# Attention blocks of 256 and 320 tokens across chunk borders in a fused attention and feed-forward kernel on one Trainium2 core

## The chip, the cores and the metric

The kernel runs on one core of one Trainium2 chip. The metric is the device time of one launch in microseconds (us); lower is better. Engines are named as the profile names them: PE is the matrix engine (PEld its weight loads), DVE the vector engine, ACT the scalar engine, POOL the GpSimd engine, and SP the queue that starts nearly all DMA transfers.

## The reference: what is computed

Attention over 8 batches, 8 heads, 576 tokens, head size 64, with keys and values first averaged over groups of eight tokens (72 pooled keys per head), and behind it a feed-forward layer over the 4608 tokens:

```python
k_p = k.reshape(B, H, Sp, pool, D).mean(axis=3)      # Sp = 72
v_p = v.reshape(B, H, Sp, pool, D).mean(axis=3)
attn = softmax(scale * q @ k_p^T)                    # 576 x 72 per head
x = (attn @ v_p), heads side by side                 # 4608 x 512
h = x @ w_in                                         # 4608 x 2048
g = h * erf(softplus(h))
out = g @ w_out                                      # 4608 x 512
```

The softmax is written here as one word; the reference has the maximum, the exponential and the sum spelled out. All is float32.

## The kernel before, in words

**Chunks and batches.** The feed-forward layer works on nine chunks of 512 tokens (`TC`), the attention on eight batches of 576. The two do not divide each other, so `blocks()` (L95) cuts the tokens of a batch into attention blocks of at most 256 tokens which end at a batch end and at a chunk end as well. That gives 24 blocks: 12 of 256 tokens, four of 192, four of 128 and four of 64. A block is made of tiles of 128 or 64 tokens.

**Attention.** `job` (L495) emits one block. Once per batch it loads and pools keys and values (L505 to L515). For each tile, `softmax_tile` loads the queries (L563), splits them into a high and a low part (L566, L571), multiplies with the keys on PE (L579, L581 or L603), does the softmax on DVE and ACT (L585 to L651), and turns the weights on PE (L658, L665) into the block's tiles `eth`, `etl` and `etb`. When all tiles of the block are there, four head pairs follow, and for each of them `values` (L690) issues **four matmuls as wide as the block** (L695), each with its own weights. The result is copied by ACT or DVE into the token buffer of the chunk (L701, L703; in chunks 0 and 1 L707, L709).

**Feed-forward.** Chunks 0 and 1 go straight: `gemm1` (L794, 12 matmuls of 512 columns for 128 of the 2048 features). From chunk 2 on (`FROM`) a Strassen scheme takes its place: `factors` (L465) makes seven combinations of the tokens of a chunk (L475, L480), `sums` (L431) makes combinations of the weights once, during chunk 1, and stores them in DRAM, and `products` (L716) reloads them through a ring of pieces of on-chip memory (L724), four pieces to two steps, and multiplies (L740, 42 matmuls of 256 columns for two steps). DVE and ACT add the products up (L758, L761, L770). Then softplus and erf on ACT (L812, L819; each switch of function loads a table), the product (L822), the split into `gh` and `gl` (L824, L829), and `gemm2` (L843, 12 matmuls of 512 columns a step). A chunk has 16 steps; `store` (L853) writes it out.

**Where things lie.** The 16 pieces `wi0` to `wi15` first hold `w_in`. When chunk 1 has used a piece, it is lent out: tokens of a chunk (`XF`), differences (`TD`), the running sum (`UU`), the sums of every other pair (`HS`), output rows (`OUT`), and the rest is the ring. With `after` an operation is held back until the first holder of its piece is done. At the start the weights come as 64-bit floats and are turned into two 32-bit parts each (`load_weights`, L370 to L408), which takes ACT, DVE and POOL; `gh`, `gl`, `hs` and the weight pieces are lent to the first batches meanwhile.

**What sets the order.** Nothing is written in its final order. Each operation has a priority in steps (`prio`) and an estimated cost, and `Program.order` (L189) places them one by one on the engines, the earliest start first with `SLACK` for priority, none more than `WINDOW` steps ahead of what PE has reached, and only if a buffer is free in the model. Some operations may go to one of several engines (`alt`). Every engine then runs its list in order. Where the model sees PE idle at the start, it puts in matmuls whose result nothing uses (L898, the fillers). The constants L39 to L76 are the priorities: of the weights (`W_IN`, `W_OUT`, `LEAD`), of pooled keys and values (`KEYS`, `VALS`), of the tiles of chunk 0 (`T0`, `T0_STEP`), of gemm2 (`G2`), of the ring (`RING_LEAD`), of `sums` (`SUMS`).

Of the kernel before, what the change touches and what calls it, by code (L numbers as in the profile page):

```python
# [37 lines left out]

WINDOW = 8  # L39
SHIFT = 3  # L40
B1 = 2
T0, T0_STEP = -10.5, 0.45
VAL_R = 2.1
KEYS, KEYS_R, KEYS_S = -5.5, 0.4, -0.5
VALS, VALS_R, VALS_S = -1.0, 0.4, -1.1
Q_DUE = 5.2
W_IN, W_OUT = 1.4, 0.1
LEAD = 4.25
G2 = 5.2
ON_DVE = 2  # L50
# [44 lines left out]
def blocks():  # L95


    out, qo = [], 0
    for b in range(B):
        t = 0  # L100
        while t < S:
            ck, off = divmod(b * S + t, TC)
            n, tiles, fresh = min(256, S - t, TC - off), [], t == 0
            for at in range(0, n, P):
                T = min(P, n - at)
                tiles.append((qo, T))
                qo += P * NP * T
            out.append((ck, b, tiles, off, fresh))
            t += n
    return out  # L110


class Buf:
# [25 lines left out]
class Program:  # L139
# [14 lines left out]
    def op(self, eng, cost, prio, fn, reads=(), writes=(), hold=(), alt=None, funcs=None, port=False):  # L154
# [135 lines left out]
def moe_attention(ctx: ExitStack, tc: tile.TileContext, cst, qa, kl, vl, wi, wo, out):  # L290
# [3 lines left out]
    if wide:  # L294
# [63 lines left out]
    def late(tag, shape, dtype=F32):  # L358
        return Buf(weights, [P] + shape, dtype, tag, [tag])
# [135 lines left out]
    def job(ck, b, tiles, off, times, first, fresh):  # L495

        base, due = times[0], times[-1] + VAL_R
        if fresh:
# [33 lines left out]
            for i in range(2):  # L532
# [150 lines left out]

        xk = xkept(ck) if ck >= FROM else xtile(ck)
        xs = slice(off, off + n)
        for p in range(NP):
# [11 lines left out]
            op("PE", 4 * max(n / 2.4 + 13, 112), r, values, [eth, etl, etb, VA, VB], [pv])  # L698
            if ck >= FROM:
                x = xk[p // 2]  # L700
                after(op("ACT", act(n, True), r + 0.4, lambda p=p, pv=pv, x=x: nc.scalar.copy(  # L701
                    x.ap[:, p % 2, xs], pv.ap[:, :n]), [pv], [(x, (p, off))],
                    alt=("DVE", dve(n), lambda p=p, pv=pv, x=x: nc.vector.tensor_copy(  # L703
                        x.ap[:, p % 2, xs], pv.ap[:, :n]))), w_in[p // 2])
                continue
            x = xk[p]
            op("ACT", act(n, True), r + 0.4, lambda x=x, pv=pv: nc.scalar.copy(  # L707
                x.ap[:, 0, xs], pv.ap[:, :n]), [pv], [(x, (0, off))])
            op("DVE", dve(n), r + 0.5, lambda x=x, pv=pv: nc.vector.tensor_sub(  # L709
                x.ap[:, 1, xs], pv.ap[:, :n], f32(x.ap[:, 0, xs])), [pv, (x, (0, off))], [(x, (1, off))])  # L710

    po = {}

    common, outs = late(UU, [4, HALF]), late(OUT, [2, DM])

    def products(n, unit, hs):  # L716
# [43 lines left out]
        multiply(n, b1, (left, "A11", "B11", True), (right, "S2", "T2", False))  # L760
        after(op("ACT", act(HALF, True), n + 0.6, lambda: nc.scalar.copy(u.ap[:, j], b1.ap[:, lo]), [b1], [(u, j)]), w_in[5])  # L761
# [4 lines left out]
        after(add(n + 0.8, c22, u0, b2, hi, [(u, j)], [(hs[1], 1)]), w_in[4])  # L766
        add(n + 0.85, c22, c22, b2, lo, [(hs[1], 1)], [(hs[1], 1)])
# [175 lines left out]
```

## Time and profile before

| | |
|---|---|
| median of 3 runs | 925.52 us (924.41 to 925.95) |
| the profiled execution, its own time | 921.54 us |
| its span, first to last instruction | 919.7 us |
| PE clock granted, mean | 0.998 |
| HBM traffic | 151.06 MB read, 24.12 MB written |

The span leaves out 1.84 us around the profiled execution. That execution was 3.98 us faster than the median of the runs. Busy times of PE are those of pipelined matmuls, so a matmul's duration is longer than its turn on the array; the distance from one start to the next is what counts.

### The profile page before, as it was taken

Reading aid. Unit: us, or ns where it says so; the run is one execution under the profiler, and the core shown is the slowest. Engines: PE = TensorE matmul, PEld = TensorE weight load, DVE = VectorE, ACT = ScalarE, POOL = GpSimd, SP = SyncE. Lnnn points to the kernel's source line nnn. Section 1 sums busy time; section 2 is a strip of 40 time slices with the busy share of each in tenths; the row PEclk is TensorE's granted clock in tenths of the full one; section 3 lists DMA queues with packets and bytes.
Section 4 is the critical chain, followed back from the end, with each engine's and each line's share of the span. In section 5 each row is a group of like instructions: output and inputs, shape, how many; then the busy total and the mean of one; then the engine's idle time right before and its main releaser. Section 6 shows DMA issues by size and latency. Waiting matters only on the chain.

```text
span 919.7 us, 16168 instructions
## 1 busy us (share of the span) xinstructions
PE 905.8 (98%) x5640; PEld 802.5 (87%) x5640; DVE 654.3 (71%) x1350; ACT 677.7 (74%) x1196; POOL 387.7 (42%) x499
## 2 busy tenths in 40 slices
PE   8999999999999999999999999999999999999998
PEld 7878788788889899999999889899998999989996
DVE  7997894889977687758667677767767866664442
ACT  4799995888668678777677777777776776766754
POOL 3679985555453345426540534344442400221000
PEclk9999999999999999999999999999999999999999
DMA  9981235256587656755665466655865365447511
GB/s 327 405 326 37 72 104 172 104 195 211 182 301 238 196 165 231 252 186 186 198 249 184 143 206 222 217 170 178 269 212 177 134 211 172 150 156 243 180 58 47
DMA packets 68257, 176.24 MB, mean 192 GB/s; under 512 B 11216, under 2 KB 13392, under 8 KB 68176
## 3 DMA queue, kind: packets, MB, share of 16 engines
q1 hardware_dynamic: 67888, 174.69, 55.8%
q8 instruction: 45, 0.74, 0.3%
q10 hardware_dynamic: 288, 0.52, 0.2%
q14 instruction: 36, 0.29, 0.1%
HBM read 151.06 MB, written 24.12 MB: 190 GB/s over the span
## 4 chain that ended last, share of the span: by engine, by line
PE 75%; DVE 6%; ACT 3%; POOL 2%; DMA 2%; issue 1%; POOLq 0%; ACTq 0%; DVEq 0%
PE banks L843 36%; PE banks L740 29%; PE banks L695 3%; PE banks L794 3%; PE banks L579 1%; PE banks L658 1%; DVE hs L822 1%; DMA w<-t 1%; PE banks L581 1%; PE banks L603 1%; ACT L812 1%; DMA wi<-w 1%; ACT y L812 1%; POOL gl L829 0%; DMA out<-f 0%
## 5 line engine op out<-in xcount | busy, mean ns | idle before, releaser
L843 PE MATMUL banks<-wo,gh 128*128 128x512 f32 x1152 | 363.8, 397 | 1.7 <-POOL wo L408 1.5
L740 PE MATMUL banks<-t,wi 128*128 128x256 f32 x2352 | 313.5, 285 | 1.9 <-DVE wi L758 1.4
L740 PEld LDWEIGHTS banks<-t,wi 128*128 128x128 f32 x2352 | 301.2, 191 | 13.4 <-DVE wi L758 2.3
L843 PEld LDWEIGHTS banks<-wo,gh 128*128 128x128 f32 x1152 | 203.9, 189 | 36.1 <-POOL wo L408 2.6
L843 PE MATMUL banks<-wo,gl 128*128 128x512 f32 x576 | 224.8, 390 | 0.0
L843 PEld LDWEIGHTS banks<-wo,gl 128*128 128x128 f32 x576 | 108.2, 188 | 23.9
L812 ACT ACT_TABLE_LOAD x72 | 92.4, 1283 | 29.5 <-DVE hs L758 13.2
L758 DVE TENSOR_TENSOR wi<-wi,banks 128x256 f32<-128x256 f32 x168 | 67.3, 413 | 37.6 <-PE banks L740 19.3
L794 PE MATMUL banks<-t,wi 128*128 128x512 f32 x384 | 93.0, 393 | 0.4 <-DVE y L822 0.4
L511 POOL TENSOR_TENSOR raw<-raw 128x256 f32<-128x256 f32 (+1 forms) x60 | 47.9, 800 | 88.5 <-DMA raw<-vl 38.4
L794 PEld LDWEIGHTS banks<-t,wi 128*128 128x128 f32 x384 | 70.9, 188 | 15.5 <-DVE y L822 0.8
L819 ACT ACTIVATE y<-y 128x1024 f32<-128x1024 f32 (+1 forms) x73 | 76.3, 1046 | 0.7
L819 ACT ACT_TABLE_LOAD x59 | 75.7, 1283 | 1.1
L569 POOL TENSOR_TENSOR ql<-raw,qh 128x512 fp32r<-128x512 f32 (+1 forms) x36 | 42.4, 1177 | 65.1 <-PE banks L843 13.2
L824 ACT CAST gh<-hs 128x512 fp32r<-128x512 f32 x72 | 44.3, 616 | 34.3 <-PE banks L843 25.2
L829 POOL TENSOR_TENSOR gl<-hs,gh 128x512 fp32r<-128x512 f32 x26 | 34.7, 1341 | 77.1 <-ACT gh L824 74.9
L822 DVE TENSOR_TENSOR hs<-y,hs 128x512 f32<-128x512 f32 x72 | 51.5, 750 | 10.8 <-ACT y L819 10.7
L829 POOL TENSOR_TENSOR gl<-wi,gh 128x512 fp32r<-128x512 f32 x20 | 25.9, 1295 | 70.7 <-ACT gh L824 51.1
L822 DVE TENSOR_TENSOR wi<-y,wi 128x512 f32<-128x512 f32 x56 | 38.0, 716 | 20.5 <-ACT y L819 20.5
L829 DVE TENSOR_TENSOR gl<-hs,gh 128x512 fp32r<-128x512 f32 x46 | 35.2, 768 | 23.1 <-ACT gh L824 22.9
L824 ACT CAST gh<-wi 128x512 fp32r<-128x512 f32 x56 | 34.3, 616 | 20.5 <-PE banks L843 13.0
L758 DVE TENSOR_TENSOR hs<-wi,banks 128x256 f32<-128x256 f32 x84 | 32.7, 416 | 22.4 <-PE banks L740 21.5
(163 smaller groups left out, 1540.8 us busy)
## 6 DMA issues: line engine op xcount, KB each, us to landing
wi<-w SPq DMA_DIRECT2D x168, 512.0 KB, 4.2
wi<-w SPq DMA_DIRECT2D x56, 256.0 KB, 4.0
raw<-vl SPq DMA_DIRECT2D x36, 256.0 KB, 3.7
wi<-wi SPq DMA_DIRECT2D x16, 512.0 KB, 8.8
wo<-wo SPq DMA_DIRECT2D x16, 512.0 KB, 8.2
w<-t SPq DMA_DIRECT2D x16, 512.0 KB, 3.4
raw<-kl SPq DMA_DIRECT2D x26, 288.0 KB, 3.4
raw<-qa SPq DMA_DIRECT2D x28, 256.0 KB, 3.9
```

The lines of the kernel that those rows point to most:

```text
L511: op("POOL", gps(4 * size), prio, lambda: nc.gpsimd.tensor_add(t.ap[:, 0:4], t.ap[:, 0:4], t.ap[:, 4:8]), [t], [t])
L569: return e.tensor_sub(ql.ap[:, :, :T], raw.ap[:, :, :T], f32(qh.ap[:, :, :T]))
L695: nc.tensor.matmul(d, w, e, start=(i == 0), stop=(i == 3), skip_group_check=True)
L740: nc.tensor.matmul(dst(), weight(name, w, p), x[:, xl, p, :], start=(first and p == 0 and q == 0), stop=(p == 1 and q == 2), skip_group_ch ...
L758: return op("DVE", dve(HALF), prio, lambda: nc.vector.tensor_add(dst(), x(), b.ap[:, side]), reads + [b], writes)
L794: nc.tensor.matmul(ph.ap, w_in[ft].ap[:, w, P * p:P * p + P], xs[p].ap[:, x], start=(p == 0 and q == 0), stop=(p == NP - 1 and q == 2))
L812: nc.scalar.activation(y.ap[:, half(k)], hh[k].ap, AF.Softplus)
L819: op("ACT", act(w), n + 1.9, lambda sl=sl: nc.scalar.activation(y.ap[:, sl], y.ap[:, sl], AF.Erf), own, own, funcs="sigmoid")
L822: op("DVE", dve(TC), n + 1.9, lambda k=k: nc.vector.tensor_mul(g(k), y.ap[:, half(k)], hh[k].ap), [(y, k), hh[k]], [gs[k]], port=kept)
L824: op("ACT", act(TC), n + 2.0, lambda k=k: nc.scalar.copy(gh[k].ap, g(k)), [gs[k]], [gh[k]], port=True, alt=("DVE", 0.52 * TC + 150, lambda ...
L829: return e.tensor_sub(gl[k].ap, g(k), f32(gh[k].ap))
L843: nc.tensor.matmul(o[t].ap, g.ap[:, gs], w_out[ft].ap[:, w], start=(ft == 0 and q == 0), stop=(ft == NJ - 1 and q == 2))
```

## The change

Four things are changed together, and with them the constants that set priorities.

1. **Blocks.** From the third batch on (`WHOLE = 2`) a batch has two blocks, one of 256 tokens and one of 320 (128 + 128 + 64), wherever the chunk borders lie. `eth`, `etl` and `etb` grow to 320 columns (`BLOCK`). A block that lies across a border is copied out of PSUM in two parts, each to the buffer of its own chunk (`parts`). 24 blocks become 18.
2. **Token buffers.** Two pairs instead of one: `wi0`, `wi1` for even chunks and `wi2`, `wi3` for odd ones. `TD` moves to `wi4`, `UU` to `wi13`, `OUT` to `wi15`, and the two `HS` share `wi14` (the class `Part`). The ring has eight pieces, `wi5` to `wi12`, instead of nine.
3. **`gl`** has two buffers instead of three, which pays for the wider tiles.
4. **Times.** A new loop, last batch first, pulls the tiles' priorities earlier, so that the last tile of a block lies `SHIFT + 4` steps ahead of its chunk and tiles lie at least `CLOSE` = 2 steps apart. The window, the priorities of the weights, of pooled keys and values, of the sums and of the ring change.

```diff
-WINDOW = 8
+WINDOW = 16
-T0, T0_STEP = -10.5, 0.45
-VAL_R = 2.1
-KEYS, KEYS_R, KEYS_S = -5.5, 0.4, -0.5
-VALS, VALS_R, VALS_S = -1.0, 0.4, -1.1
+T0, T0_STEP = -10.5, 0.55
+VAL_R = 4.0
+KEYS, KEYS_R, KEYS_S = -6.5, 0.4, -0.7
+VALS, VALS_R, VALS_S = -0.5, 0.4, -0.7
-W_IN, W_OUT = 1.4, 0.1
-LEAD = 4.25
-G2 = 5.2
+W_IN, W_OUT = 0.9, -0.8
+LEAD = 4
+G2 = 5.0
-SLACK, BIAS = 30, 1150
+SLACK, BIAS = 34, 1150
-RING = tuple(f"wi{i}" for i in range(7, NJ))
-XF, TD, UU, HS, OUT = ("wi0", "wi1"), "wi2", "wi5", ("wi3", "wi4"), "wi6"
-SUMS, SUMS_R = 4.3, 0.3
+RING = tuple(f"wi{i}" for i in range(5, 13))
+XF, TD, UU, HS, OUT = ((0, 1), (2, 3)), 4, 13, 14, 15
+WHOLE, CLOSE, BLOCK = 2, 2.0, 320
+SUMS, SUMS_R = 0.5, 2.3
-RING_LEAD = 6.25
+RING_LEAD = 7.25
...
             n, tiles, fresh = min(256, S - t, TC - off), [], t == 0
+            if b >= WHOLE:
+                n = S - t if t else 256
...
-             "s": 2, "m": 2, "z": 2, "bb": 1, "ks": 1, "vs": 1, "hs": 3, "y": 1, "f": 2, "gh": 3, "gl": 3}
+             "s": 2, "m": 2, "z": 2, "bb": 1, "ks": 1, "vs": 1, "hs": 3, "y": 1, "f": 2, "gh": 3, "gl": 2}
...
-            xf[ck] = [late(XF[i], [2, TC]) for i in range(2)]
+            xf[ck] = [late(f"wi{i}", [2, TC]) for i in XF[ck % 2]]
...
-        r = NJ * (FROM - 1) + 2 * i + SUMS
+        r = NJ * (FROM - 1) + SUMS_R * i + SUMS
...
-        xk = xkept(ck) if ck >= FROM else xtile(ck)
-        xs = slice(off, off + n)
+        parts, at = [], 0
+        while at < n:
+            k, o = divmod(TC * ck + off + at, TC)
+            w = min(n - at, TC - o)
+            parts.append((k, slice(o, o + w), slice(at, at + w)))
+            at += w
...
+    soon = None
+    for ck, b, tiles, off, times, _, _ in reversed(jobs):
+        for i in reversed(range(len(tiles))):
+            if b >= WHOLE:
+                times[i] = min(times[i], NJ * ck - 4 - SHIFT - CLOSE * (len(tiles) - 1 - i))
+                if soon is not None:
+                    times[i] = min(times[i], soon - CLOSE)
+                soon = times[i]
```

Since the order is computed, three places of it are shown as it stands before and after.

PE, batch 3, before: the 64 tokens at the end of chunk 3 (`eth`, `etl`, `etb` are turned softmax weights, `vah`, `val`, `vb` pooled values). Two of the four head pairs:

```order
L695 MATMUL banks<-eth,vah 128x64
L695 MATMUL banks<-etl,vah 128x64
L695 MATMUL banks<-eth,val 128x64
L695 MATMUL banks<-etb,vb 64x64
L843 MATMUL banks<-wo_1655,gh 128x512 x2
L843 MATMUL banks<-wo_1655,gl 128x512
L843 MATMUL banks<-wo_1655,gh 128x512 x2
L843 MATMUL banks<-wo_1655,gl 128x512
L695 MATMUL banks<-eth,vah 128x64
L695 MATMUL banks<-etl,vah 128x64
L695 MATMUL banks<-eth,val 128x64
L695 MATMUL banks<-etb,vb 64x64
```

PE, the same place after: the same 64 tokens and the 256 that follow them in chunk 4 (L714 is the former L695, L866 the former L843, L762 the former L740):

```order
L714 MATMUL banks<-eth,vah 128x320
L714 MATMUL banks<-etl,vah 128x320
L714 MATMUL banks<-eth,val 128x320
L714 MATMUL banks<-etb,vb 64x320
L866 MATMUL banks<-wo_1532,gh 128x512 x2
L866 MATMUL banks<-wo_1532,gl 128x512
L866 MATMUL banks<-wo_1532,gh 128x512 x2
L866 MATMUL banks<-wo_1532,gl 128x512
L762 MATMUL banks<-t,wi_3949 128x256 x6
L714 MATMUL banks<-eth,vah 128x320
L714 MATMUL banks<-etl,vah 128x320
L714 MATMUL banks<-eth,val 128x320
```

What were two blocks with 16 matmuls each is one block with 16 wider ones.

POOL at the start, before: from the first pair's `gl` to the low part of the second `w_out` piece, `wo1` (L332 and L408 are conversions, L390 the low bits of a weight):

```order
L829 TENSOR_TENSOR gl_1038<-y_933,gh_1031 128x512
L829 TENSOR_TENSOR gl_1048<-y_933,gh_1042 128x512
L332 TENSOR_SCALAR wo0_1080<-f_1050 128x512
L390 TENSOR_SCALAR hs_1085<-wi5_646 128x512
L408 TENSOR_TENSOR wo0_1080<-f_1050,wo0_1080 128x512
L675 TENSOR_SCALAR etb_1087<-etb_1087 32x2x128
L547 TENSOR_TENSOR vb_128<-f_898,vb_128 32x256
L332 TENSOR_SCALAR wi4_1126<-f_1114 128x512
L408 TENSOR_TENSOR wi4_1126<-f_1114,wi4_1126 128x512
L511 TENSOR_TENSOR raw_1054<-raw_1054 128x288
L408 TENSOR_TENSOR wo1_1152<-f_1128,wo1_1152 128x512
```

POOL, the same stretch after (L852 is the former L829, L423 the former L408, L347 and L405 the former L332 and L390):

```order
L423 TENSOR_TENSOR wo0_934<-f_923,wo0_934 128x512
L662 TENSOR_TENSOR bb_986<-s_845,z_887 128x64
L666 TENSOR_TENSOR s_845<-s_845,z_887 128x576
L347 TENSOR_SCALAR vb_128<-f_938 128x256
L852 TENSOR_TENSOR gl_1032<-y_920,gh_1026 128x512
L852 TENSOR_TENSOR gl_1045<-y_920,gh_1037 128x512
L423 TENSOR_TENSOR wi4_1049<-f_1040,wi4_1049 128x512
L690 TENSOR_SCALAR etb_1081<-etb_1081 32x2x128
L405 TENSOR_SCALAR hs_1092<-wo3_727 128x512
L562 TENSOR_TENSOR vb_128<-f_938,vb_128 32x256
L347 TENSOR_SCALAR wo1_1114<-f_1096 128x512
L423 TENSOR_TENSOR wo1_1114<-f_1096,wo1_1114 128x512
```

`wo0` has moved ahead of the `gl` pair; behind that pair five operations stand ahead of the low part of `wo1`, where eight stood.

PE at the end of batch 7, after: the last value matmul of the kernel, and, behind what the dots leave out, the first two products of chunk 8, which need it (`t` are the token factors):

```order
L714 MATMUL banks_9888<-eth_9351,val_127 128x320
L714 MATMUL banks_9888<-etb_9326,vb_128 64x320
...
L866 MATMUL banks_9272<-wo11_1735,gh_9870 128x512 x2
L866 MATMUL banks_9272<-wo11_1735,gl_9921 128x512
L866 MATMUL banks_9276<-wo11_1735,gh_9870 128x512 x2
L866 MATMUL banks_9276<-wo11_1735,gl_9921 128x512
L762 MATMUL banks_9991<-t_9932,wi5_9839 128x256 x6
L762 MATMUL banks_9991<-t_9935,wi7_9853 128x256 x6
```

The dots stand for 18 matmuls of gemm2 and 30 products of chunk 7; with the six shown, 24 of gemm2 and 30 products lie between the last value matmul and the first product of chunk 8. Before, 36 of gemm2 and 60 products lay there.

More of the change, by code (lines that the diff above doesn't have):

```diff
@@ L129, in ap, with __init__ @@
         return self._ap
+class Part:
+    def __init__(self, whole, at):
+        self.whole, self.at, self.state = whole, at, {}
+    @property
+    def ap(self):
+        return self.whole.ap[:, self.at]
 class Op:
@@ L167, in op @@
                 buf, key = a if isinstance(a, tuple) else (a, None)
-                if isinstance(buf, Buf) and buf not in o.bufs:
-                    o.bufs.append(buf)
+                whole = buf.whole if isinstance(buf, Part) else buf
+                if isinstance(whole, Buf) and whole not in o.bufs:
+                    o.bufs.append(whole)
                 for k, (writer, readers) in buf.state.items():
@@ L467, in factors @@
         x0, x1 = xkept(ck)
-        d = late(TD, [2, 2, HALF])
+        d = late(f"wi{TD}", [2, 2, HALF])
         r = NJ * ck - X_DUE
@@ L481, in split @@
                 u.ap[:, 1], src(), f32(u.ap[:, 0])), [acc, (u, 0)], [(u, 1)])
-        after(sub(0, one, b12, b11, [x0], [(d, 0)]), w_in[2])
+        after(sub(0, one, b12, b11, [x0], [(d, 0)]), w_in[TD])
         sub(1, b12, b22, b12, [x0, x1], [(x0, "t3")])
@@ L551, in job @@
         second = ck == 0 and off > 0 and wide
-        eth, etl, etb = (loan(LENT_E[i], sh, F32R) if second else buf(t, sh, F32R) for i, (t, sh) in
-                         enumerate((("eth", [NP, 256]), ("etl", [NP, 256]), ("etb", [2, 256]))))
+        eth, etl, etb = (loan(LENT_E[i], [sh[0], 256], F32R) if second else buf(t, sh, F32R) for i, (t, sh) in
+                         enumerate((("eth", [NP, BLOCK]), ("etl", [NP, BLOCK]), ("etb", [2, BLOCK]))))
         bank = lambda kind: Buf(banks, [P, 512], F32, "banks", ["banks", "att0" if ck == 0 else kind])
@@ L698, in job @@
             op("PE", 4 * max(n / 2.4 + 13, 112), r, values, [eth, etl, etb, VA, VB], [pv])
[L699 to L710, printed above, removed]
+            for k, xs, ps in parts:
+                w = ps.stop - ps.start
+                if k >= FROM:
+                    x = xkept(k)[p // 2]
+                    after(op("ACT", act(w, True), r + 0.4, lambda p=p, pv=pv, x=x, xs=xs, ps=ps: nc.scalar.copy(
+                        x.ap[:, p % 2, xs], pv.ap[:, ps]), [pv], [(x, (p, xs.start))],
+                        alt=("DVE", dve(w), lambda p=p, pv=pv, x=x, xs=xs, ps=ps: nc.vector.tensor_copy(
+                            x.ap[:, p % 2, xs], pv.ap[:, ps]))), w_in[XF[k % 2][p // 2]])
+                    continue
+                x = xtile(k)[p]
+                op("ACT", act(w, True), r + 0.4, lambda x=x, pv=pv, xs=xs, ps=ps: nc.scalar.copy(
+                    x.ap[:, 0, xs], pv.ap[:, ps]), [pv], [(x, (0, xs.start))])
+                op("DVE", dve(w), r + 0.5, lambda x=x, pv=pv, xs=xs, ps=ps: nc.vector.tensor_sub(
+                    x.ap[:, 1, xs], pv.ap[:, ps], f32(x.ap[:, 0, xs])),
+                   [pv, (x, (0, xs.start))], [(x, (1, xs.start))])
     po = {}
-    common, outs = late(UU, [4, HALF]), late(OUT, [2, DM])
+    common, outs = late(f"wi{UU}", [4, HALF]), late(f"wi{OUT}", [2, DM])
     def products(n, unit, hs):
@@ L760, in products @@
         multiply(n, b1, (left, "A11", "B11", True), (right, "S2", "T2", False))
-        after(op("ACT", act(HALF, True), n + 0.6, lambda: nc.scalar.copy(u.ap[:, j], b1.ap[:, lo]), [b1], [(u, j)]), w_in[5])
+        after(op("ACT", act(HALF, True), n + 0.6, lambda: nc.scalar.copy(u.ap[:, j], b1.ap[:, lo]), [b1], [(u, j)]), w_in[UU])
         u0, c12, c21, c22 = ((lambda: u.ap[:, j]), (lambda: hs[0].ap[:, hi]), (lambda: hs[1].ap[:, lo]),
@@ L765, in products @@
         multiply(n + 0.3, b2, (left, "S1", "T1", True), (right, "S3", "T3", False))
-        after(add(n + 0.8, c22, u0, b2, hi, [(u, j)], [(hs[1], 1)]), w_in[4])
+        after(add(n + 0.8, c22, u0, b2, hi, [(u, j)], [(hs[1], 1)]), w_in[HS])
         add(n + 0.85, c22, c22, b2, lo, [(hs[1], 1)], [(hs[1], 1)])
@@ L772, in products @@
         for o in (first, add(n + 1.2, c12, u0, b2, lo, [(u, j)], [(hs[0], 1)])):
-            after(o, w_in[3])
+            after(o, w_in[HS])
         add(n + 1.2, c21, u0, b2, hi, [(u, j)], [(hs[1], 0)])
@@ L781, in pair @@
         if units[0][0] >= FROM and n // 2 % 2:
-            hs = [late(HS[k], [TC]) for k in range(2)]
+            whole = late(f"wi{HS}", [2, TC])
+            hs = [Part(whole, k) for k in range(2)]
         if units[0][0] >= FROM:
@@ L856, in store @@
             kept = common if t == 2 else outs
-            key, piece = (kept, ("out", t)), w_in[5 if t == 2 else 6]
+            key, piece = (kept, ("out", t)), w_in[UU if t == 2 else OUT]
             at = lambda: kept.ap[:, 2:4].rearrange("p a f -> p (a f)") if t == 2 else kept.ap[:, t]
```

## Prediction

> **What bounds the kernel now.** I read the busy times by stage first, then PE's waits, then the groups of instructions, then the timeline where a price was wanted. By stage (PE, PEld, DVE, ACT, POOL busy, then granted clock, DMA share, GB/s):
>
> ```profile
> 0.00:46.00 46.00, 42.06 (x331) 35.88 (x331) 37.94 (x90) 28.89 (x106) 23.12 (x35) 1.00 0.98 365
> 46.00:69.00 23.00, 20.93 (x124) 17.18 (x124) 22.13 (x45) 20.77 (x37) 17.64 (x21) 1.00 0.85 326
> 69.00:230.00 161.00, 159.53 (x780) 131.66 (x779) 130.39 (x247) 137.37 (x233) 112.96 (x137) 1.00 0.38 128
> 230.00:276.00 46.00, 44.38 (x258) 38.69 (x257) 38.30 (x83) 31.02 (x56) 22.12 (x31) 0.96 0.71 243
> 276.00:575.00 299.00, 298.71 (x1973) 271.43 (x1971) 215.29 (x452) 222.90 (x389) 121.83 (x165) 1.00 0.61 204
> 575.00:897.00 322.00, 321.65 (x2095) 292.30 (x2094) 204.82 (x429) 226.85 (x364) 88.78 (x111) 1.00 0.54 180
> ```
>
> From 276 to 897 us PE is idle for 0.64 of 621 us, with DVE at 68%, ACT at 72%, and DMA at 0.54 to 0.61. There the time is the PE work, matmul by matmul. Before that PE is not full, mainly in three places: 3.94 us idle up to 46, 2.07 us up to 69 (where DVE is at 96%, and DMA at 0.85), and 1.62 us from 230 to 276, where the granted clock is 0.96. PE's own waits say for whom:
>
> ```profile
> PE banks L898 <- DMA cst<-cst: 2.6, 1, 2.6
> PE banks L843 <- POOL wo L408: 1.5, 1, 1.5
> PE banks L740 <- DVE wi L758: 1.4, 1, 1.4
> ```
>
> The first is the start itself. No wait names a ring load, `gl`, or a token factor.
>
> **Part 1, the blocks: PE work goes away.** A block costs 16 value matmuls whatever its width. The price of one is the distance between starts, so I take first and last rows of runs from the timeline: a block of 64 up to the next gemm1; four of a 192 block in a row, up to gemm2; a block of 128; eight of a 256 block.
>
> ```profile
> 52.67 0.28 PE L695 MATMUL banks<-eth,vah 128*128 128x64 f32 x1
> ...
> 54.29 3.00 PE L794 MATMUL banks<-t,wi 128*128 128x512 f32 x12
> ...
> 138.59 0.25 PE L695 MATMUL banks<-eth,vah 128*128 128x192 f32 x1
> ...
> 138.99 0.65 PE L843 MATMUL banks<-wo,gh 128*128 128x512 f32 x2
> ...
> 216.38 0.22 PE L695 MATMUL banks<-eth,vah 128*128 128x128 f32 x1
> ...
> 217.92 0.68 PE L843 MATMUL banks<-wo,gh 128*128 128x512 f32 x2
> ...
> 305.64 0.28 PE L695 MATMUL banks<-eth,vah 128*128 128x256 f32 x1
> ...
> 306.60 0.63 PE L843 MATMUL banks<-wo,gh 128*128 128x512 f32 x2
> ```
>
> So 16 of 64 columns take 1.62 us, of 128 columns 1.54, of 192 columns 4 x 0.40 = 1.60, of 256 columns 2 x 0.96 = 1.92. From 64 to 192 columns the price hardly moves. The gemm2 behind a narrow group starts a little late too (0.65 and 0.68 for its first two, where 0.62 and 0.63 are usual), so I take 1.60 for 128 and 1.70 for 192. For 320 columns the trace has nothing; below it lie 256 columns, above it the 512 of gemm1 and gemm2:
>
> ```profile
> 228.59 0.62 PE L843 MATMUL banks<-wo,gh 128*128 128x512 f32 x2
> ...
> 231.31 2.88 PE L794 MATMUL banks<-t,wi 128*128 128x512 f32 x12
> ```
>
> Twelve of 512 in 2.72 us are 0.227 each; 256 columns are 0.120 each; a quarter of the way is 0.147, or 2.35 us for 16 (bounds: 0.135, a little over 256, and 0.155). Batches 2 to 7 had nine blocks of 256 and three each of 192, 128 and 64: 9 x 1.92 + 3 x (1.70 + 1.60 + 1.62) = 32.0 us. They get six of 256 and six of 320: 6 x 1.92 + 6 x 2.35 = 25.6. **That takes 6.4 us off PE** (5.5 to 7.5 by the bounds), all of it in the stage where PE waits for nobody.
>
> So a 64-column matmul with weights of its own takes 1.62 / 16 = 0.10 us. [...]
>
> Nothing else of the attention shrinks: the 40 tiles keep their scores, softmax and turns. The copies out of PSUM go from 72 to 68 in these batches (five of the twelve blocks are copied in two parts), on engines with a third of their time free: nothing.
>
> **Part 2, the start.** Up to 69 us PE is ahead of the conversion of weights. PE and POOL where the 1.5 us wait lies:
>
> ```profile
> 60.27 1.28 POOL L408 TENSOR_TENSOR wo<-f,wo 128x512 fp32r<-128x512 f32 x1
> ...
> 62.99 0.68 POOL L332 TENSOR_SCALAR wi<-f 128x512 fp32r<-128x512 f32 x1
> 63.75 1.28 POOL L408 TENSOR_TENSOR wi<-f,wi 128x512 fp32r<-128x512 f32 x1
> ...
> 64.78 0.42 PE L603 MATMUL banks<-kbd,qh 128*128 128x144 f32 x2 [0.41 <-DVE s L625]
> ...
> 65.39 0.80 POOL L511 TENSOR_TENSOR raw<-raw 128x288 f32<-128x288 f32 x1 [0.36 <-DMA wo<-wo]
> ...
> 65.48 0.44 PE L843 MATMUL banks<-wo,gh 128*128 128x512 f32 x1
> ...
> 66.15 1.27 POOL L408 TENSOR_TENSOR wo<-f,wo 128x512 fp32r<-128x512 f32 x1
> 67.47 0.51 PE L843 MATMUL banks<-wo,gh 128*128 128x512 f32 x1 [1.55 <-POOL wo L408]
> ```
>
> The second `wo` ends at 67.42 and PE goes on at 67.47. In the new order the low part of `wo0` (1.28) stands ahead of the `gl` pair, the key pooling (0.80) behind `wo1`, and of three copies like that at 62.99 (0.68) two are left out and one is new. From the pair on, `wo1` has 1.28 + 0.80 + 0.68 = 2.8 us less ahead of it. PE, too, asks for it earlier, since the six score matmuls from 64.78 to 65.48 (0.7 us) come behind it now. About 2 us remain, more than the wait, and I take the 1.5 us as gone. There are ten fewer fillers (202 for 212):
>
> ```profile
> L898 PE MATMUL banks<-cst 128*128 128x256 bf16 x212 | 27.3, 291 | 2.6 <-DMA cst<-cst 2.6
> ```
>
> At 27.3 / 212 = 0.13 us they are 1.3 us, but they stand in for waiting, and go only if DVE and DMA, both full there, let PE start earlier. I count nothing for them, and 1.5 us for the start. At best all idle time but the first 2.6 goes, and the fillers: 6.0 - 2.6 + 1.3 = 4.7. At worst, since all weights, keys and values have new due times and are queued on SP in a new order, one transfer more stands ahead of a wanted one; a weight piece takes 8.2 us to land, and half of that, 4, is my bound:
>
> ```profile
> wo<-wo SPq DMA_DIRECT2D x16, 512.0 KB, 8.2
> ```
>
> **Part 3, the change-over to products.** At 262 PE waits for a PSUM bank that DVE has not added up yet, and the next products run slowly:
>
> ```profile
> 262.20 3.40 PE L740 MATMUL banks<-t,wi 128*128 128x256 f32 x18 [1.40 <-DVE wi L758]
> ...
> 266.21 2.21 PE L740 MATMUL banks<-t,wi 128*128 128x256 f32 x12
> ...
> 299.68 2.52 PE L740 MATMUL banks<-t,wi 128*128 128x256 f32 x18 [0.29 <-DVE z L641]
> ```
>
> 18 products take 3.40 us here and 2.52 at 299.68; with the clock at 0.96 over 46 us, 1.8 us of PE turns were lost, and 1.6 to idling: 3.4 in all. [...] The change moves `sums` about four steps earlier and sets gemm2 between shorter runs of products, so there is more time for DVE's adds; but the running sum `UU` now lies in a piece (`wi13`) that `sums` frees late. I take 1.0 off; bounds 3.4 off and, if one such wait is added, 1.7 on.
>
> **Part 4, what it pays with.** *Ring of eight:* a load is issued when its piece is free, lands in 4.2 us, and PE never waits for one:
>
> ```profile
> wi<-w SPq DMA_DIRECT2D x168, 512.0 KB, 4.2
> SPq L724 <- PE banks L740: 322.8, 163, 7.6
> ```
>
> Eight pieces are two pairs of steps; a pair is 42 x 0.120 + 24 x 0.227 = 10.5 us of PE, which covers 4.2. Nothing; without that cover, each of 56 pairs would wait. *Two `gl`:* the third `gl` let a conversion start while two were still being read. Now DVE or POOL waits for gemm2 of the pair before (24 x 0.227 = 5.4 us), with what stands behind on DVE, the adds of L758 among it, for which PE's next products wait. Today DVE waits for ACT there, not for PE:
>
> ```profile
> DVE gl L829 <- ACT gh L824: 45.4, 36, 2.7
> ```
>
> PE waits for none of it, and a conversion on DVE is 0.69 us; I count 1.0 us on for all of part 4, the start's two `gl` for three included; bounds 0 and 4. *The new priorities* take 26 operations off POOL, most of them for DVE (some 20 us in all at 0.7 to 0.8 each), which has 32% of 621 us free: nothing.
>
> **The sum.** -6.4 - 1.5 - 1.0 + 1.0 = -7.9 us: the profiled execution's 921.54 us become 913.6 (span 919.7 to 911.8), and the median 925.52, which lies 3.98 higher, **917.6 us**.
>
> **The rivals.**
>
> *Chunk borders take the place of what is saved (slower).* The last block of a batch now brings its tokens in one lump. In the new order 24 matmuls of gemm2 and 30 products lie between it and the first product of chunk 8: 24 x 0.227 + 30 x 0.120 = 9.0 us, where it was 36 and 60, 15.4 us. Within that, DVE and ACT must copy the tokens, make the factors and split them. For it: 15.4 may have been needed. Against it: at chunk 3 PE had only 7.0 us between the last values and the first product, and no wait stands there:
>
> ```profile
> 333.91 0.22 PE L695 MATMUL banks<-etb,vb 96*64 96x64 f32 x1
> ...
> 340.90 1.67 PE L740 MATMUL banks<-t,wi 128*128 128x256 f32 x12
> ```
>
> It decides where the chain takes more than 9 us. At 2 us for each of seven borders, 14 us go on: 917.6 + 14 = 931.6. It turns the result slower from 7.9 / 7 = 1.1 us a border. Chance 0.10.
>
> *The start gives it back (about the same).* DVE and DMA are full there, so a new order of loads can cost its upper bound: -6.4 + 4 + 1.0, no gain in part 3: -1.4, or 924.1 us. Chance 0.13, a third of it faster by the measure below, a seventh slower.
>
> *Columns, not weight loads, set the price.* [...]
>
> ```profile
> 328.63 0.19 PE L695 MATMUL banks<-eth,vah 128*128 128x64 f32 x1
> ...
> 328.94 0.71 PE L843 MATMUL banks<-wo,gh 128*128 128x512 f32 x2
> ```
>
> Chance 0.02.
>
> *Start and change-over both clear up.* -6.4 - 4.7 - 3.4 + 0.5 = -14.0: 911.5 us. Chance 0.05.
>
> That the blocks are not merged is excluded: the order shows 96 fewer value matmuls.
>
> **How the numbers follow.** The forecast has 0.70. Of the range, the low end is the last rival, 911.5; the high end is the forecast with the bounds of start and part 4 (917.6 + 5.5 + 3 = 926), less 1 since both at once is unlikely: 925. That leaves out the borders and some of the unlikely sums, under 2 in 10. About 0.2% (1.85 us) is what a measurement of this kernel can tell from no change. Faster by more: 0.70 less 0.01 for its upper end, 0.05, and 0.04 of the start: 0.78. Slower: 0.10 and 0.02: 0.12. Within: 0.10.
>
> **What would show it.** Right: 96 matmuls fewer at the values' line, 16 of 320 columns in 2.3 to 2.4 us, PE idle under 1.5 us in the 600 us before the tail, no wait for `wo` near 65 us. The border rival shows as PE waits for `t` at the first products of a chunk; the `gl` cost as PE waits for DVE's adds or for `gl`; a bad start as more idle before 69 us. The forecast is wrong if the values' matmuls of 64 columns cost less in the batches than in the rows above, or if new waits of over 6 us stand on PE.

## The result, and the profile after

| | before | after |
|---|---|---|
| median | 925.74 us (924.41 to 926.62, 4 runs) | 913.20 us (912.94 to 914.27, 4 runs) |
| the profiled execution, its own time | 921.54 us | 914.27 us |
| its span | 919.7 us | 912.5 us |

After is faster: the ratio is 0.9868, with a 95% interval of 0.9851 to 0.9885. The forecast was 917.6 us. Note the two differences: 12.5 us between the medians, but 7.3 us between the profiled executions. They are taken apart below. One execution of the kernel before, of 2283.87 us, is the only slow one on record and is left out of every comparison.

The changed kernel by stage, with the columns of the first fence of the prediction:

```profile
0.00:46.00 46.00, 40.13 (x316) 34.05 (x316) 36.98 (x90) 29.24 (x107) 23.15 (x36) 1.00 0.97 356
46.00:69.00 23.00, 21.53 (x124) 17.25 (x122) 20.43 (x41) 21.43 (x38) 19.09 (x23) 1.00 1.03 408
69.00:230.00 161.00, 158.22 (x773) 130.20 (x774) 135.61 (x276) 135.39 (x237) 103.98 (x130) 0.99 0.38 130
230.00:276.00 46.00, 46.00 (x273) 40.94 (x272) 38.59 (x78) 35.55 (x58) 21.09 (x29) 1.00 0.62 212
276.00:575.00 299.00, 298.04 (x1938) 270.67 (x1937) 217.16 (x465) 221.53 (x377) 120.30 (x166) 1.00 0.62 207
575.00:890.00 315.00, 314.98 (x2028) 286.14 (x2027) 203.07 (x420) 224.46 (x360) 74.09 (x92) 1.00 0.53 181
```

The change-over (230 to 276) has become a stretch with no idle PE and full clock: 46.00 of 46, where it was 44.38 at 0.96. The start has not gained: PE is idle for 5.87 us up to 46, where it was 3.94. From 276 on PE is still full: idle for 0.98 us up to 890. PE's largest waits after, in us in total, times, and the longest:

```profile
PE banks L680 <- POOL bb L662: 3.4, 5, 1.3
PE banks L929 <- DMA cst<-cst: 2.6, 1, 2.6
PE banks L618 <- POOL ql L584: 1.6, 1, 1.6
...
PE banks L866 <- POOL wo L423: 0.2, 1, 0.2
```

The wait for the low part of `wo` has gone from 1.5 to 0.2, and the wait for DVE's adds is gone. In their place PE waits for POOL: for the turned weights' `bb` (2.2 of the 3.4 us lie before 46 us) and, at 69 us, for a tile's `ql`.

**A measure for what follows.** Busy time hides small losses, so the distance from each matmul to the next start is compared with what that shape usually takes (0.227 us for 512 columns, 0.120 for 256, and so on). The usual distances sum to PE's work, the rest is lost time. PE's work is 887.3 us before and 880.1 after: 6.1 from the value matmuls and 1.1 from ten fewer fillers. Lost time by stage, in us, one profiled execution each (0 to 130 is the start, 130 to 230 chunk 1, 230 to 276 the change-over):

| kernel | 0-69 | 69-130 | 130-230 | 230-276 | from 276 |
|---|---|---|---|---|---|
| before | 9.7 | 1.5 | 2.4 | 4.7 | 7.1 |
| before, once more | 10.6 | 1.5 | 2.5 | 5.3 | 8.3 |
| after | 11.3 | 3.5 | 4.1 | 0.2 | 6.6 |
| after, once more | 12.4 | 3.5 | 4.1 | 0.2 | 6.6 |
| old cut | 10.5 | 3.5 | 5.9 | 1.5 | 8.3 |
| new sums in before | 10.5 | 1.5 | 5.2 | 1.1 | 9.0 |
| old start | 7.7 | 1.0 | 11.0 | 0.1 | 14.1 |
| old lag | 8.8 | 5.3 | 15.0 | 0.8 | 17.1 |
| two `gl` in before | 9.3 | 7.0 | 3.1 | 3.6 | 10.7 |
| refit | 10.5 | 0.7 | 4.4 | 1.1 | 8.5 |

### The profile page after: what moved, and what is told of

The parts are those of the page before. It is cut to its first block, busy times and chain, and to the rows that moved or that the text cites. A ratio compares the mean times of both kernels' runs of the same rounds, so it can differ in the third digit from the quotient of the medians.

```text
span 912.5 us, 15938 instructions
## 1 busy us (share of the span) xinstructions
PE 897.5 (98%) x5534; PEld 794.6 (87%) x5534; DVE 658.6 (72%) x1378; ACT 677.7 (74%) x1190; POOL 361.8 (40%) x473
## 4 chain that ended last, share of the span: by engine, by line
PE 80%; DVE 3%; ACT 2%; POOL 2%; issue 1%; POOLq 0%; ACTq 0%
PE banks L866 39%; PE banks L762 30%; PE banks L817 4%; PE banks L714 3%; PE banks L594 1%; PE banks L673 1%; PE banks L596 1%; DVE hs L845 0%; PE banks L618 0%; PE banks L680 0%; DVE t L475 0%; DVE f L465 0%; ACT L835 0%; POOL raw L528 0%; POOL raw L526 0%
## 5 line engine op out<-in xcount | busy, mean ns | idle before, releaser
L866 PE MATMUL banks<-wo,gh 128*128 128x512 f32 x1152 | 363.8, 397 | 0.2 <-POOL wo L423 0.2
L762 PEld LDWEIGHTS banks<-t,wi 128*128 128x128 f32 x2352 | 303.0, 191 | 11.9
L762 PE MATMUL banks<-t,wi 128*128 128x256 f32 x2352 | 310.3, 283 | 0.0
L866 PEld LDWEIGHTS banks<-wo,gh 128*128 128x128 f32 x1152 | 202.4, 189 | 32.4 <-POOL wo L423 0.6
L866 PE MATMUL banks<-wo,gl 128*128 128x512 f32 x576 | 225.0, 391 | 0.0
L866 PEld LDWEIGHTS banks<-wo,gl 128*128 128x128 f32 x576 | 108.2, 188 | 24.2
L817 PE MATMUL banks<-t,wi 128*128 128x512 f32 x384 | 94.9, 399 | 1.0 <-DVE y L845 0.9
L852 POOL TENSOR_TENSOR gl<-hs,gh 128x512 fp32r<-128x512 f32 x24 | 32.5, 1353 | 77.1 <-PE banks L866 31.1
L852 DVE TENSOR_TENSOR gl<-hs,gh 128x512 fp32r<-128x512 f32 x48 | 34.4, 716 | 38.5 <-PE banks L866 36.0
L847 ACT CAST gh<-wi 128x512 fp32r<-128x512 f32 x56 | 34.6, 619 | 25.7 <-PE banks L866 15.7
L852 DVE TENSOR_TENSOR gl<-wi,gh 128x512 fp32r<-128x512 f32 x38 | 27.1, 713 | 32.9 <-PE banks L866 32.4
L600 ACT COPY s<-banks 128x144 f32<-128x144 f32 x100 | 25.5, 280 | 26.0 <-PE banks L596 25.7
```

The lines of the kernel that those rows point to most:

```text
L762: nc.tensor.matmul(dst(), weight(name, w, p), x[:, xl, p, :], start=(first and p == 0 and q == 0), stop=(p == 1 and q == 2), skip_group_ch ...
L817: nc.tensor.matmul(ph.ap, w_in[ft].ap[:, w, P * p:P * p + P], xs[p].ap[:, x], start=(p == 0 and q == 0), stop=(p == NP - 1 and q == 2))
L847: op("ACT", act(TC), n + 2.0, lambda k=k: nc.scalar.copy(gh[k].ap, g(k)), [gs[k]], [gh[k]], port=True, alt=("DVE", 0.52 * TC + 150, lambda ...
L852: return e.tensor_sub(gl[k].ap, g(k), f32(gh[k].ap))
L866: nc.tensor.matmul(o[t].ap, g.ap[:, gs], w_out[ft].ap[:, w], start=(ft == 0 and q == 0), stop=(ft == NJ - 1 and q == 2))
```

## The experiments

The theory after the result: PE's work fell by what the blocks save, and the change-over cleared because `sums` moved earlier. The first rival: the new numbers do it, and the blocks little. The second: no part does it by itself, and the gain beyond the blocks is how the whole order fits.

**before_again: the kernel before, unchanged.**

> The kernel before, unchanged, to see how far one execution of it stands from another: its profiled execution took 921.5 us, its four timed runs 924.4 to 926.6. If the difference lies at the change-over to products (a wait of 1.4 us and 3.4 us of half clock were there, 3.4 us lost in all), a second profile shows PE idle from 230 to 276 us of more than 1.6 us, or a clock under 0.96 there. If it lies at the start, PE is idle for more than 6.0 us before 69 us. If neither, both profiles agree stage by stage and the runs differ outside the span. Ratio to itself 1.000 within 0.002.

924.29 us (12 runs, 921.19 to 926.45) beside 924.47, ratio 0.9999 (0.9987 to 1.001). The profiled execution took 924.40 and shows the same places. Three of them lose more: the start 0.9 us, the change-over 0.6 (PE waits there 2.16 us instead of 1.40), and the stretch from 276 on 1.2. So an execution of this order takes between 921 and 927 us, and the one that the prediction worked from, 921.54, was at the bottom.

**after_again: the changed kernel, unchanged.**

> The changed kernel, unchanged, on the chip of its neighbours here: 913.2 us within 0.2% (911.4 to 915.0). Its profile should again show a start up to 69 us that loses about 11 us beyond the PE work, one stretch of half clock near 71 us, and next to nothing from 230 to 276 us. If these two places move, they are a matter of the single execution, and not of the order.

913.57 us (912.73 to 915.28), ratio 0.9885 (0.9872 to 0.9898). The stages repeat to 0.1 us from 69 us on. One thing does not: the half clock. The same wait for `ql`, then 24 matmuls of gemm1, and then gemm2, first in the first execution of after:

```profile
69.44 0.34 PE L618 MATMUL banks<-kbd,ql 128*128 128x144 f32 x1 [1.64 <-POOL ql L584]
...
69.94 7.31 PE L817 MATMUL banks<-t,wi 128*128 128x512 f32 x24
77.09 0.61 PE L866 MATMUL banks<-wo,gh 128*128 128x512 f32 x2
```

and in the second:

```profile
70.61 0.34 PE L618 MATMUL banks<-kbd,ql 128*128 128x144 f32 x1 [1.64 <-POOL ql L584]
...
71.11 5.67 PE L817 MATMUL banks<-t,wi 128*128 128x512 f32 x24
76.61 0.62 PE L866 MATMUL banks<-wo,gh 128*128 128x512 f32 x2
```

From 69.94 to 77.09 are 7.15 us, from 71.11 to 76.61 are 5.50. The wait is 1.64 us both times; only in the first did the clock drop behind it, for 3.4 us, at a cost of 1.65. The stage from 69 to 130 us, first in the first execution and then in the second:

```profile
69.00:130.00 61.00, 59.61 (x279) 48.93 (x280) 51.38 (x92) 55.43 (x89) 51.20 (x60) 0.97 0.30 104
```

```profile
69.00:130.00 61.00, 57.40 (x274) 46.66 (x275) 51.33 (x90) 55.43 (x88) 51.53 (x60) 1.00 0.32 108
```

With the full clock (1.00 for 0.97) PE is only idle for longer, 3.60 us for 1.39; DVE, ACT and POOL do the same in both, and the lost time is 3.5 both times. So one expected part failed: the half clock near 71 us belongs to the execution. The losses belong to the order: PE waits for the other engines here, and gives no time away by being slow.

**narrow: blocks of at most 128 tokens from the third batch on.**

```diff
-                n = S - t if t else 256
+                n = min(P, S - t)
```

> The changed kernel with blocks of at most 128 tokens from the third batch on: 30 blocks in those batches instead of 12, the same columns in all. By the weight load: 6 x (4 x 1.60 + 1.62) = 48.1 us of value matmuls instead of 25.6, so 913.2 + 22.5 = 935.7 us. [...]

941.16 us, ratio 1.0179 (1.0159 to 1.02): 28.0 us over the changed kernel. In place of 12 blocks there are 30, with the same columns in all. Here are four value matmuls of 128 columns and the product behind them:

```profile
412.84 0.22 PE L714 MATMUL banks<-eth,vah 128*128 128x128 f32 x1
...
413.19 1.65 PE L762 MATMUL banks<-t,wi 128*128 128x256 f32 x12
```

Four take 0.35 us, and four of 320 columns take 0.59:

```profile
332.40 0.31 PE L714 MATMUL banks<-eth,vah 128*128 128x320 f32 x1
...
332.99 0.62 PE L866 MATMUL banks<-wo,gh 128*128 128x512 f32 x2
```

Summed over all its rows, a block of 128 costs 1.46 us, one of 64 costs 1.36, and the matmul behind each group starts late by 0.19 a block: 24 x 1.46 + 6 x 1.36 + 30 x 0.19 = 48.9, where six of 256 and six of 320 take 6 x 1.92 + 6 x 2.38 = 25.8. That is 23.1 of the 28.0 us; the rest is new waits, the longest of them 2.1 us for POOL's `bb`, 1.8 for ACT and 1.2 for DVE's adds. So with the same columns it is the number of value matmuls that sets the price; columns tell only in the wide ones, 1.92 us a block at 256 and 2.38 at 320.

**old_cut: blocks cut as before, everything else new.**

```diff
-            if b >= WHOLE:
-                n = S - t if t else 256
```

> The changed kernel with the blocks cut as before (24 instead of 18), all else kept. If each value matmul costs its weight load, PE gets 6.4 us of work back: 913.2 + 6.4 = 919.6 us. [...] If the cut also carries part of the rest (fewer, larger lumps of tokens that the model places better), more than 7.5 us: above 920.7.

925.63 us, ratio 1.0014 (1.0004 to 1.0025), the last of the expected results. Without the blocks nothing is left of the gain: the new buffers, ring and numbers are worth nothing alone. It is 12.4 us above the changed kernel, and the price of the blocks is 6.4 of these. Of the rest the table shows 4.8 as losses in the last three stages (15.7 for 10.9). The largest is one wait of PE:

```profile
175.71 0.40 PE L592 MATMUL banks<-kbd,qh 128*128 128x288 f32 x1 [2.69 <-ACT f L883]
```

Scores of a tile wait there for ACT's copy of finished output rows, a wait that after does not have.

**new_numbers: the kernel before with the new window, weights, keys, values and lags.**

```diff
-WINDOW = 8
+WINDOW = 16
-T0, T0_STEP = -10.5, 0.45
-VAL_R = 2.1
-KEYS, KEYS_R, KEYS_S = -5.5, 0.4, -0.5
-VALS, VALS_R, VALS_S = -1.0, 0.4, -1.1
+T0, T0_STEP = -10.5, 0.55
+VAL_R = 4.0
+KEYS, KEYS_R, KEYS_S = -6.5, 0.4, -0.7
+VALS, VALS_R, VALS_S = -0.5, 0.4, -0.7
...
-SLACK, BIAS = 30, 1150
+SLACK, BIAS = 34, 1150
```

(`W_IN`, `W_OUT`, `LEAD` and `G2` move too.)

> The kernel before with the new window, slack and priorities of weights, keys, values, tiles of chunk 0 and gemm2, all else as before. If these numbers help by themselves (as the 14.8 us that they are worth in the changed kernel may suggest): below 920 us. If they only fit the new blocks and buffers: 924 or more. The forecast took 1.5 us for them at the start: 922.9.

925.78 us, ratio 1.0011 (0.9999 to 1.0023): nothing. The first rival falls here, for all numbers but those of `sums`, which new_sums tries below, and of the ring, which old_cut has new as well.

**old_numbers: the changed kernel with those numbers back** (the same diff, turned round).

> The changed kernel with the window, slack and the priorities of weights, keys, values, tiles of chunk 0 and gemm2 set back to those of before; blocks, buffers, ring, sums and the pull of the tiles stay. If the numbers help at the start as forecast (1.5 us): 914.7. If they cost there, as the trace of the change has it (fillers aside some 3 us more lost before 130 us), about 910. If the numbers, not the blocks, carry the gain beyond 6.4 us, about 6 us more: 919.

927.98 us, ratio 1.0046 (1.0029 to 1.0062), 14.8 us above the changed kernel, although its blocks are the wide ones, and far above all three expected results. PE's largest single wait:

```profile
277.90 7.05 PE L762 MATMUL banks<-t,wi 128*128 128x256 f32 x42 [3.33 <-DVE wi L780]
```

The change-over's wait is back, and longer: 3.33 us, where the two executions of before had 1.40 and 2.16. So the blocks' saving of 6.4 us can be spent twice over by the order around it.

**old_start: only the numbers of the start back.**

```diff
-T0, T0_STEP = -10.5, 0.55
+T0, T0_STEP = -10.5, 0.45
-KEYS, KEYS_R, KEYS_S = -6.5, 0.4, -0.7
-VALS, VALS_R, VALS_S = -0.5, 0.4, -0.7
+KEYS, KEYS_R, KEYS_S = -5.5, 0.4, -0.5
+VALS, VALS_R, VALS_S = -1.0, 0.4, -1.1
-W_IN, W_OUT = 0.9, -0.8
-LEAD = 4
+W_IN, W_OUT = 1.4, 0.1
+LEAD = 4.25
```

> The changed kernel with only the numbers of the start set back (tiles of chunk 0, keys, values, weights and their lead); window, slack, value lag and gemm2 stay new. The trace of the change loses 4 to 5 us more before 230 us than that of before, and has 1.1 us fewer fillers. If the start's numbers do that, about 910 us; if they help as forecast, 914.7; if they are what the change-over and chunk 1 need too, above 918.

925.09 us, ratio 1.0002 (0.999 to 1.0014). This one teaches most of the start. Up to 130 us it loses 8.7 us, where after loses 14.8; but it has 3.3 us more of fillers there (25.3 for 22.0), which stand in for waiting. The new start is the worse one by about 3 us. From 130 us on, though, old start loses 25.2, where after loses 10.9. Its PE waits there:

```profile
PE banks L762 <- DVE wi L780: 3.0, 6, 1.1
...
PE banks L594 <- ACT f L885: 1.8, 2, 1.4
PE banks L866 <- POOL gl L852: 1.3, 1, 1.3
```

The new numbers give about 3 us away at the start, and what is placed behind it fits.

**old_lag: only the lag from a block's last tile to its value matmuls back.**

```diff
-VAL_R = 4.0
+VAL_R = 2.1
```

> The changed kernel with the lag between a block's last tile and its value matmuls back from 4.0 to 2.1 steps (VAL_R), and nothing else changed. If that lag is what keeps the waits out of chunk 1 and the change-over with the wider blocks: 918 us or more, with PE waiting for ACT or DVE at the values or the products behind them. If it is a number like the others that only has to fit at the start: 913 to 915 us.

938.80 us, ratio 1.0152 (1.0134 to 1.0169): 25.2 us above the changed kernel beside it, the dearest undo. The expected place is only half right: PE waits at the products (3.9 us for DVE's adds), but hardly at the values (0.3). The longest wait is at a score matmul, at 137.91, whose PSUM bank DVE has still to read:

```profile
134.68 0.23 PE L596 MATMUL banks<-kbd,ql 128*128 128x144 f32 x1
137.91 0.40 PE L594 MATMUL banks<-kbd,qh 128*128 128x288 f32 x1 [3.00 <-DVE y L845]
```

The same stretch, first on DVE and then on ACT:

```profile
134.01 0.50 DVE L349 CAST wo<-f 128x512 fp32r<-128x512 f32 x1
137.17 0.69 DVE L845 TENSOR_TENSOR y<-y,banks 128x512 f32<-128x512 f32 x1 [2.66 <-ACT y L842]
```

```profile
132.39 1.28 ACT L835 ACT_TABLE_LOAD   x1
133.68 1.09 ACT L835 ACTIVATE y<-banks 128x512 f32<-128x512 f32 x2
134.79 1.28 ACT L842 ACT_TABLE_LOAD   x1
136.08 1.06 ACT L842 ACTIVATE y<-y 128x1024 f32<-128x1024 f32 x1
```

Softplus and erf of a pair take ACT 4.7 us with their table loads, 1.28 us each. DVE's product stands behind them, the score's bank behind that, and PE behind the bank. In after the scores around this place, from 128.47 to 132.07 us, wait for nothing. A lag of values moves no work, but it decides what stands behind such a chain. Not every switch of function on ACT loads a table: in before each of the 72 softplus runs does, but only 59 of the 72 erf runs; the other 13 stand behind the softmax's function at L634, which loaded one.

**gl2_before: the kernel before with two `gl`.**

```diff
-             ... "gh": 3, "gl": 3}
+             ... "gh": 3, "gl": 2}
```

> The kernel before with two gl buffers instead of three, and nothing else changed. Part 4 of the prediction put the loss of the third gl at up to 1 us with the rest of the ring costs, with bounds 0 and 4. If that is right: 925 to 926 us where the kernel before takes 924.7. The rival theory, that the third gl is dear in the old order and the changed kernel only escapes the price because its numbers were chosen with two: 928 us or more, with new waits of PE for gl, or behind it for DVE's adds.

931.58 us, ratio 1.0073 (1.006 to 1.0086): 7.4 us, far more than forecast; the rival theory holds for the old order. How long DVE and POOL sat idle before an operation on `gl`, with the largest entry of each list (until whom, us in total, times), in before, in this kernel, and in after:

```profile
  ACT gh L824: 171.4, 49
```

```profile
  PE banks L843: 83.3, 58
```

```profile
  PE banks L866: 130.7, 73
```

With three, the conversions wait for their input. With two, they wait for gemm2, as the prediction said. But that alone is not the price: in after, DVE and POOL wait even longer for gemm2, 130.7 us, and no wait of PE for `gl` stands in its list. The 7.4 us come from the order that is computed around it, at 96 to 107 us above all:

```profile
96.36 0.45 PE L603 MATMUL banks<-kbd,qh 128*128 128x144 f32 x2 [1.57 <-DVE f L402]
...
98.54 8.14 PE L794 MATMUL banks<-t,wi 128*128 128x512 f32 x24 [1.13 <-DVE s L625]
```

No wait there is for `gl`; 24 matmuls take 8.14 us instead of 5.5, since the clock is at half for 6.8 us from 96.9 on.

**new_sums: the kernel before with only `sums` moved.**

```diff
-        r = NJ * (FROM - 1) + 2 * i + SUMS
+        r = NJ * (FROM - 1) + 2.3 * i + 0.5
```

> The kernel before with nothing changed but the due times of the weight sums (from step 0.5 of chunk 1 on and 2.3 steps apart, instead of from 4.3 on and 2.0 apart). Theory: PE's wait at the change-over (1.4 to 2.3 us, and half clock behind it; 4.7 to 5.3 us lost from 230 to 276) comes from the sums being late, so that DVE is behind with its adds when products begin. Then about 4 us go: 924.4 - 4 = 920.4 us, with less than 1.5 us lost there. Rival: it comes from where the running sum and the ring lie, or from the window and priorities; then 924.4 within 0.2%, and the wait stays.

922.98 us, ratio 0.9984 (0.9971 to 0.9998): 1.9 us faster, just clear of no change, and half of what was expected. Chunk 1 and the change-over:

```profile
130.00:230.00 100.00, 96.86 (x483) 80.06 (x482) 82.05 (x172) 76.65 (x137) 51.00 (x66) 1.00 0.48 167
230.00:276.00 46.00, 46.00 (x277) 40.30 (x276) 37.11 (x77) 32.48 (x59) 24.29 (x36) 1.00 0.64 219
```

The change-over clears (46.00 at clock 1.00, lost time 4.7 to 1.1), and chunk 1 pays back 2.8; PE waits there for `gl`, 1.54 us at 171.50 and 0.82 at 184.10. So `sums` is what cleared it here.

**old_sums: the changed kernel with `sums` where it was.**

```diff
-SUMS, SUMS_R = 0.5, 2.3
+SUMS, SUMS_R = 4.3, 2.0
```

> The changed kernel with the due times of the weight sums set back. If the sums carry the gain at the change-over: 913.2 + 4 = 917 us, with a wait for a DVE add near 260 us. If the buffers, the window or the priorities carry it: 913.2 within 0.2%. A third way: the running sum lies in a piece that the last sums free, so later sums hold up the first product: more than 5 us on.

914.75 us, ratio 0.9888 (0.9872 to 0.9905), 1.5 us above the changed kernel. The intervals of the two ratios touch, so this is at the edge of what can be told. Its change-over loses 1.9 us and its chunk 1 2.1, where after has 0.2 and 4.1. In the new order the late `sums` do not bring the wait for DVE's adds back; PE waits 1.6 us for POOL's `gl` at 271.05 instead. The time of `sums` was enough to clear that wait in before, but is not needed in after.

**refit: eight numbers of the changed kernel moved a little.**

```diff
-T0, T0_STEP = -10.5, 0.55
+T0, T0_STEP = -11.0, 0.55
...
-LEAD = 4
+LEAD = 3.5
...
-SUMS, SUMS_R = 0.5, 2.3
-X_DUE = 2.6
-RING_LEAD = 7.25
+SUMS, SUMS_R = 0.0, 2.7
+X_DUE = 2.9
+RING_LEAD = 6.25
```

(`KEYS_S` and `VALS_S` go to -1.1.)

> The changed kernel with eight of its numbers moved a little (first tiles 0.5 steps earlier, keys and values of later batches closer together, weights half a step later, sums half a step earlier and spread wider, token tiles and ring shifted). Blocks, buffers and PE work stay the same. Theory: beyond the 7.2 us of PE work, the gain is the fit of the whole order, and a neighbouring set of numbers can fit as well or better, mostly by losing less before 69 us: 910 to 913 us. Rival: the changed kernel's numbers are a narrow best, and moving several of them brings waits in chunk 1 (130 to 230 us) as every undo did: 917 us or more.

914.74 us, ratio 0.9896 (0.9882 to 0.9909), beside 913.57 for the changed kernel: the same within the intervals, and neither of the two expected results. It loses 0.7 us at 69 to 130 instead of 3.5, and gives that back at the change-over and behind. No version here beats the changed kernel.

## Why the prediction was right, and where it was not

**Part 1, the blocks (-6.4): right, in mechanism and size.** A block of 320 took 2.38 us (forecast 2.35). The rows of all blocks behind 200 us give 9 x 1.92 + 3 x (1.67 + 1.52 + 1.33 + 0.45) = 32.2 before, where 0.45 is what the matmuls behind three narrow blocks lose, and 25.8 after: 6.4. By the usual distances it is 6.1. narrow shows the same price with the sign turned, which settles the columns rival. No run shows a price by columns alone: narrow has the columns of after, and its blocks cost 48.9 us for 25.8. The rows beside that rival, of four matmuls of 64 columns, are 0.31 us, or 0.08 for each, where four of 320 take 0.59. One detail was off: the prediction called itself wrong if matmuls of 64 columns cost less in the batches than its row of 1.62 us a block, and they do, 1.33. The matmul behind such a group starts late and takes most of this back, so the three narrow widths together cost 4.97 where 4.92 was forecast.

**Part 2, the start (-1.5): wrong sign.** The step that held is the one wait it was worked from: `wo`, 1.5 to 0.2. The step that failed is to take that wait as what the start loses. The order behind it is computed anew, so POOL's `bb` (up to 130 us: 0.6 and 1.9 us in the two executions of before, 2.2 and 3.1 in those of after) and `ql` (none, then 1.6) came in its place. Over two executions of each kernel the start lost, up to 130 us, (11.2 + 12.1) / 2 = 11.7 before and (14.8 + 15.9) / 2 = 15.4 after: +3.7, just inside the bound of 4. For the fillers I counted nothing, and 1.1 us of them went.

**Part 3, the change-over (-1.0): right place, too small.** It gave (4.7 + 5.3) / 2 - 0.2 = 4.8, more than the bound of 3.4, since that bound was what the first execution lost to one wait and the clock behind it, and the stretch lost more than that beside them. 18 products run at full speed now, 2.32 us where they took 3.40; the distance from their start to the gemm2 behind them is 2.15:

```profile
258.88 2.32 PE L762 MATMUL banks<-t,wi 128*128 128x256 f32 x18
261.03 0.63 PE L866 MATMUL banks<-wo,gh 128*128 128x512 f32 x2
```

No wait of PE names the running sum in `wi13`.

**Part 4, ring, `gl` and priorities (+1.0): not paid in after.** PE waits there neither for a ring load nor for `gl`, and from 276 on loses 6.6 us, where it lost 7.1 and 8.3. But 1.0 as the price of a `gl` was wrong as a general price: 7.4 us in the old order, above the bound of 4. Chunk 1, to which the prediction gave no term, lost 1.6 more (4.1 for 2.5).

**The sum.** By parts, as the two pairs of executions show it: -6.1 - 1.1 + 3.7 - 4.8 + 1.6 - 1.1 (from 276 on) = -7.8 us, beside -7.9. Against the forecast the parts missed by 7.1 us upwards (start 5.2, chunk 1 1.6, blocks 0.3) and by 7.0 downwards (change-over 3.8, part 4 2.1, fillers 1.1). Beyond the term of the blocks, the agreement of the sum is luck.

**The median.** This is why 917.6 became 913.2. The sum was made against an execution of 921.54 us and moved to the median by 3.98 us, as if the changed kernel's profiled execution would lie as far below its median. It lay 1.07 above. Within the sum the miss is 914.27 - 913.6 = +0.6; the offset makes 3.98 + 1.07 = 5.0 the other way, together -4.4. The offset was itself large because 925.52 is the median of three: the 74 readings of before in the series of before_again, old_start and gl2_before have a median of 924.32, 2.8 above 921.54. The readings of before lie between 921.19 and 927.34, those of after between 912.73 and 915.28. Why the old order varies more is settled only in part. Of the 74 readings, the nine at a granted clock of 1.000 have a median of 923.0 us, the 32 at 0.998 one of 924.3, and the 17 at 0.996 one of 925.5, so some 2.5 us go with the clock; each of these groups still spreads over 3.4 to 5 us, and only two executions were profiled.

**The rivals.** Chunk borders: no wait of PE for `t` at the first products of a chunk stands among its waits in after. The start did give back 3.7, but the change-over's 4.8, which that rival had set to nothing, met it. Start and change-over both clear: half of it came.

**What carries the gain.** Neither half of the change does alone: new numbers and buffers with old blocks 925.63, new blocks with old numbers 927.98, both 913.20. The series of after_again gives 924.22 and 913.57, a gain of 10.7 us where the first gave 12.5. Of this, 7.2 are PE's work. The waits add little in the profiled pairs: behind 130 us after loses 4.3 us less ((14.2 + 16.1) / 2 - 10.9), and up to 130 us 3.7 more. The other 3 to 5 us between the medians lie in executions that were not profiled, and no trace shows where. That the order has to fit as a whole is what the undos show: each but that of `sums` made the kernel slower by 6 to 25 us beyond the blocks' price, in other places each time. Not tried alone: a third `gl` beside the wide blocks, and the loop that pulls the tiles earlier.

## What to carry to other kernels

Price the work that an edit removes from the distance between starts; that term held to a few tenths of a microsecond. Where an order is computed, do not price the waits one by one: a wait removed is replaced by another that the trace of before cannot name, so give such parts a range with both signs, and test an undo of each group of numbers, since one alone (a lag of 2 steps) was worth 25 us. Profile the kernel before more than once before working from its span: here its executions lay 6 us apart.

## What the runs showed of the hardware

The half clock (0.50 in the clock records of the traces) came in stretches of 3.4 or 6.8 us, at or behind waits of PE of 1.4 to 3.3 us, and behind the same wait of 1.64 us in one execution of after and not in the other. In the first execution of after it lasted 3.413 us, from 71.14 us on, behind the wait that ended at 69.44; in the first of before also 3.413, from 264.07 on, behind the wait of 1.40 that ended at 262.20. Each of the two has one more drop, in its last microseconds: at 910.82 in after, 839.68 us or 246.0 such lengths behind the first, and at 919.43 in before, 655.36 us or 192.0 lengths behind. What decides whether a wait brings a drop is not shown.

A drop of 3.4 us cost 24 matmuls of gemm1 1.65 us, and where PE waits for other engines anyway, as in the start of after, it cost the kernel nothing that can be seen.
